# Second products four steps behind the first during the attention units, weights prepared three instructions a step, low-part products last

## The chip, the cores and the metric

One core of one Trainium2 chip runs the whole kernel. The time is the device time of one execution in microseconds (us); lower is better. TensorE (PE) does the matrix products, VectorE (DVE), ScalarE (ACT) and GpSimd (POOL) the elementwise work, SyncE (SP) issues the transfers. Each engine takes its instructions in the order in which the program gives them.

## What is computed

A decaying linear attention over 2 batches, 8 heads, 768 positions and 64 columns, and then two pairs of dense layers (512 to 2048 to 512) on its 1536 rows. In short, from the reference:

```python
state = gamma * state + outer(k[:, :, t], v[:, :, t])      # per head, for each t
y[:, :, t] = scale * q[:, :, t] @ state
h = x @ w_in;  g = max(h, 0) + log1p(exp(-abs(h)));  x = g @ w_out        # first pair
h = x @ w_in;  g = s * max(h, 0)**2 + b;             out = g @ w_out      # second pair
```

## The kernel before, in words

**Attention.** The sequence is cut into 12 chunks of 128 positions; a *unit* n is half the heads of chunk n // 2, so there are 24. For each unit PE makes the scores (`att_scores`, line 168), DVE multiplies them with the decay mask (line 172, tile `a`), and PE makes the output and the state's update (`att_out`, line 184). ACT copies the output as rounded high part into `xh` (line 216), DVE takes the rest into `xl` (line 222), adds up the state (lines 237 and 239), ACT copies that (lines 248 and 255).

**Layers.** Every number is held as a high and a low part, and a product of two such numbers is three products: high by high, high by low, low by high. A *step* s takes one block of 128 hidden columns (f4 of 4 in a group) for 512 rows (j of 3): `h_mm(s)` (line 313) is 12 products into one PSUM bank, the first products. `act_0` to `act_lo` make the activation of it (DVE line 322, ACT line 333, DVE line 338, ACT line 356 into `gh`, POOL or DVE line 360 into `gl`). `acc_mm` (line 376) is the second products, 12 of them, three into each of four banks (`acc01` is one tile of two banks, `acc2` and `acc3` are one each); four steps of a group add up in the same banks. After the fourth, `take_out` copies the four banks out (for the first group on ACT, line 382), and the next group may only then begin in them. There are 96 steps.

**Weights.** A tile of weights arrives as one transfer of 512 KB (`raw`, issued by `load_next` on SP in the third of its four preparing instructions) and is prepared by `split_w`: DVE instructions on lines 277, 281, 286 and 292, an ACT square on line 284, then ACT copies the high part `wh` (line 106) and POOL subtracts for the low part `wl` (line 109). The first four pieces are the first-product weights of f4 = 0 to 3, used by steps 0 to 3; then come the second-product weights in the same order. `fill(n)` issues the next n of these pieces, four to a tile.

**Order.** It is written out by hand. Units 0 to 7 run first (two tiles of weights are prepared there). Then eight steps carry two units each: steps 0 to 2 by `early` (first products, unit, scores, unit, scores, `fill(4)` at the end), steps 3 to 7 by `mixed`, which also has the second products of step s - 3 between the two units (`LAG_U = 3`) and calls `fill(2)` twice. In `early` the second unit's output lies in bank `acc3` and half of the scores in `acc01`. After the units one step's second products are made up, and the steady steps follow, 88 of them, each with the first products of s and the second products of s - 2 (`LAG`).

First products of a step up to 7 always use one bank `h`, so `h_mm(s + 1)` can start when `act_2(s)` (DVE, line 338) has read it. The weights' pool holds six tiles of each kind, the pool `raw` four transfers, the pool of `gh` and `gl` LAG_U + 1 pairs.

Of the kernel before, what the change touches and what calls it, by code (L numbers as in the profile page):

```python
# [13 lines left out]
P = 128  # L14
# [10 lines left out]
KC = DM // P  # L25
NF = DFF // P
FG = 4
# [4 lines left out]
WARM = {"first": 6, "u0": 3, "s2": 1}  # L32
FIRST, SECOND = (0, 1), (2, 3)
LAG = 2
LAG_U = 3
TINY_SQ = float.fromhex("0x1.44p-30")
HF = 2
HP = NP // HF
# [7 lines left out]
def tile_retention_mlps(ctx: ExitStack, tc: tile.TileContext, qk, kv, w1, w2, sb, consts, out):  # L46
    nc = tc.nc
# [2 lines left out]
    inp = ctx.enter_context(tc.tile_pool(name="inp", bufs=NIN))  # L50
    scp = ctx.enter_context(tc.tile_pool(name="scaled", bufs=2))
    ap_ = ctx.enter_context(tc.tile_pool(name="att", bufs=3))
    rawp = ctx.enter_context(tc.tile_pool(name="raw", bufs=4))
    dp = ctx.enter_context(tc.tile_pool(name="dec", bufs=2))
    wp = ctx.enter_context(tc.tile_pool(name="w", bufs=RING))
    gp = ctx.enter_context(tc.tile_pool(name="g", bufs=LAG_U + 1))
    tp = ctx.enter_context(tc.tile_pool(name="t", bufs=2))
    ps_acc = ctx.enter_context(tc.tile_pool(name="ps_acc", bufs=1, space=bass.MemoryType.PSUM))
    ps_h = ctx.enter_context(tc.tile_pool(name="ps_h", bufs=1, space=bass.MemoryType.PSUM))
    ps_y = ctx.enter_context(tc.tile_pool(name="ps_y", bufs=1, space=bass.MemoryType.PSUM))  # L60
    ps_s = ctx.enter_context(tc.tile_pool(name="ps_s", bufs=1, space=bass.MemoryType.PSUM))

    def bank(pool, tag):
        return pool.tile([P, 512], F32, tag=tag, name=tag)

    def sums():

        t = ps_acc.tile([P, 2, 512], F32, tag="acc01", name="acc01")
        return [t[:, 0], t[:, 1], bank(ps_acc, "acc2"), bank(ps_acc, "acc3")], t
# [14 lines left out]
    xh = [cp.tile([P, KC, TT], F32R, tag=f"xh{j}", name=f"xh{j}") for j in range(NTILE)]  # L84
    xl = [cp.tile([P, KC, TT], F32R, tag=f"xl{j}", name=f"xl{j}") for j in range(NTILE)]
# [10 lines left out]
    def word():  # L96
        if fill.at >= LAG_U:
            return dp.tile([P, DM], F32, tag="wx", name="wx", bufs=1)
        return ac[2]
# [201 lines left out]
    steps = [(la, g, j, f4) for la in range(2) for g in range(NG) for j in range(NTILE) for f4 in range(FG)]  # L301
    h_t, l_t, gg_t, acc_t = {}, {}, {}, {}

    def h_mm(s, part):
        la, g, j, f4 = steps[s]
        wh, wl = w_t[la * NF + g * FG + f4, 0]
        if part == 0:
            h_t[s] = bank(ps_h, "h") if s < SB or s % 2 else bank(ps_y, "y")
        ps = h_t[s]
        for cc in (0, 1) if part == 0 else (2, 3):  # L310
            wa, wb = (w[:, cc * P : (cc + 1) * P] for w in (wh, wl))
            for i, (l, r) in enumerate(((wa, xh), (wa, xl), (wb, xh))):
                nc.tensor.matmul(  # L313
                    ps, l, r[j][:, cc, :], start=cc == 0 and i == 0, stop=cc == KC - 1 and i == 2
                )

    def act_0(s):
        ps = h_t[s]
# [43 lines left out]
    def acc_mm(s, banks):  # L362
        la, g, j, f4 = steps[s]
        wh, wl = w_t[la * NF + g * FG + f4, 1]
        gh, gl = gg_t[s]
        if (la, g, j) not in acc_t:
            acc_t[la, g, j] = sums()[0] if acc_t else ac
        for cc in banks:
            cs = slice(cc * P, (cc + 1) * P)
            ps = acc_t[la, g, j][cc]  # L370
            if la == 0:
                ops = ((wh[:, cs], gh), (wh[:, cs], gl), (wl[:, cs], gh))
            else:
                ops = ((gh[:, cs], wh), (gh[:, cs], wl), (gl[:, cs], wh))
            for i, (l, r) in enumerate(ops):
                nc.tensor.matmul(ps, l, r, start=f4 == 0 and i == 0, stop=f4 == FG - 1 and i == 2)  # L376

    def take_out(s, cc):
        la, g, j, f4 = steps[s]
# [17 lines left out]
    SB = (NU - N0) // HF  # L397
# [5 lines left out]
    def slot_free(w, i):  # L403
# [6 lines left out]
            if x[0] >= FG  # L410
            else (-2, 2 * (x[0] + (LAG_U if x[1] else 0)) + x[1])
        ),
# [5 lines left out]
    def load_next():  # L418
        x = next(loads, None)
        if x:  # L420
            load_w(*x)
# [53 lines left out]
    def out_of(y):  # L475
        return y[:, :HC], y[:, HC : HC + HP * D]
# [3 lines left out]
    def fill(n):  # L480

        for _ in range(n):
            if not left[0]:
                if nxt[0] is None or fill.at < slot_free(*nxt[0]):
                    return
                work[0] = split_w(*nxt[0], pause=False)
                nxt[0] = next(splits, None)
                left[0] = 4
            next(work[0], None)
            left[0] -= 1  # L490

    with tc.manual_schedule():
        fill.at = -1
        nc.scalar.preload_act_table_set("softplus")
        nc.vector.memset(zero, 0.0)
        nc.vector.memset(st, 0.0)
        nc.vector.memset(cu[:, 0:1], 0xC0000000)
        nc.vector.memset(cu[:, 1:2], 29)
        load_qk(0)
        nc.sync.dma_start(out=cst[:, :CG], in_=consts[:, :CG])  # L500
        load_kv(0)
        nc.sync.dma_start(out=cst[:, CG:], in_=consts[:, CG:])
        load_qk(1)
        load_kv(1)
        load_qk(2)
        load_next()
        load_kv(2)
        load_qk(3)
        load_kv(3)

        def warm(bank, key):
            for _ in range(WARM[key]):
                nc.tensor.matmul(bank[:, 0:P], zero[:, 0:P], zero[:, P : 2 * P], start=True, stop=True)

        ys = [bank(ps_h, "h"), bank(ps_y, "y")]
        warm(ac[3], "first")
        scale_q(0)
        scale_v(0)
        score_to(2, lent)
        warm(ac[3], "u0")  # L520
        for n in range(N0):
            if n >= len(ys):
                ys.append(bank(*((ps_h, "h"), (ps_y, "y"))[n % 2]))
            unit(n, out_of(ys[n]))
            if n == 1:
                load_next()
                load_next()
                nc.sync.dma_start(out=sbt, in_=sb)
                warm(ac[3], "s2")

            score_to((2, 4, 5, 6, 7, 8, 9, 10)[n], lent)
            fill((0, 0, 0, 1, 1, 1, 1, 4)[n])

        def early(s):

            fill.at = s
            n = N0 + HF * s
            h_mm(s, 0)
            h_mm(s, 1)
            act_0(s)  # L540
            unit(n, out_of(bank(ps_y, "y")), lambda: act_1(s))
            score_to(n + 3, lent)
            act_2(s)
            act_3(s)
            unit(n + 1, out_of(ac[3]))
            act_hi(s)
            score_to(n + 4, lent)
            fill(4)
            act_lo(s, nc.gpsimd)

        def mixed(s):

            old = s - LAG_U
            fill.at = s
            n = N0 + HF * s
            h_mm(s, 0)
            h_mm(s, 1)
            act_0(s)
            unit(n, out_of(bank(ps_y, "y")), lambda: act_1(s))
            score_to(n + 3, own)  # L560
            act_2(s)
            act_3(s)
            act_hi(s)
            fill(2)
            acc_mm(old, FIRST)
            acc_mm(old, SECOND)
            unit(n + 1, out_of(bank(ps_y, "y")))
            score_to(n + 4, own)
            act_lo(s, nc.gpsimd)
            if steps[old][3] == FG - 1:  # L570
                for cc in range(KC):
                    take_out(old, cc)
            fill(2)

        for s in range(SB):
            (early if s < LAG_U else mixed)(s)
        for old in range(SB - LAG_U, SB - LAG):
            acc_mm(old, FIRST)
            acc_mm(old, SECOND)
        fill(left[0])  # L580
        work = iter(())
        for s in range(SB, NS + LAG):
            run, old, prev = s < NS, s - LAG, s <= NS
            takes = steps[old][3] == FG - 1
            late = work
            work = split_next(s + 1) if run and not takes else iter(())
            if run:
                h_mm(s, 0)
                h_mm(s, 1)
                act_0(s)  # L590
            if prev and s > SB:
                act_3(s - 1)
            go(work, 2)
            if run:
                acc_mm(old, FIRST)
                if takes:
                    take_out(old, 0)
                    take_out(old, 1)
                act_1(s)
            if prev and s > SB:  # L600
                act_hi(s - 1)
            if run:
                act_2(s)
            go(late, 1)
            if prev and s > SB:
                act_lo(s - 1)
            if run:
                acc_mm(old, SECOND)
                if takes:
                    take_out(old, 2)  # L610
                    take_out(old, 3)
            go(work, 2)

        for banks in (FIRST, SECOND[:1], SECOND[1:]):
            for old in (NS - 2, NS - 1):
                acc_mm(old, banks)
            for cc in banks:
                take_out(NS - 1, cc)
# [70 lines left out]
```

## Time and profile before

| | us |
|---|---|
| median of three runs | 586.97 (586.72 to 587.11) |
| the profiled execution | 587.33 |
| its span, first to last instruction | 585.2 |
| TensorE busy | 574.6 (98%) |
| VectorE, ScalarE, GpSimd busy | 452.4, 223.1, 134.9 |

The profile is one execution. The timeline lists instructions with their start, their duration and, in square brackets, how long the engine had been idle and which instruction ended that. The chain of waits follows the work that ended last back to its beginning. A product's duration in the timeline is longer than the step from one product to the next, because products overlap.

### The profile page before, as it was taken

The numbers are of one execution on the slowest core, as the hardware profiler recorded it, in microseconds if no ns is written. First come the engines' busy times: TensorE is split into PE (matmuls) and PEld (weight loads), VectorE is DVE, ScalarE is ACT, GpSimd is POOL, SyncE is SP. The second block draws the span as 40 slices with busy tenths as digits, with TensorE's granted clock in tenths as the row PEclk, the third lists the DMA queues.
The fourth block names the chain that finished last, engine by engine and source line by source line (L and its number), as shares of the span: only waits on it lengthen the run. The fifth ranks groups of instructions, "written<-read, shape, count | busy, mean of one in ns | idle before, by whom it ended". The sixth has DMA issues, their size and how long they took to land.

```text
span 585.2 us, 7908 instructions
## 1 busy us (share of the span) xinstructions
PE 574.6 (98%) x3028; PEld 472.7 (81%) x3028; DVE 452.4 (77%) x692; ACT 223.1 (38%) x441; POOL 134.9 (23%) x110
## 2 busy tenths in 40 slices
PE   8899999999999999999999999999999999999997
PEld 7776778888888888888778888888888888888885
DVE  4888665679999997899869897878778876874553
ACT  3655653443333333333534532333333332332121
POOL 3447632021021120121433420121101110110000
PEclk9999999999999999999999999999999999999999
DMA  8985212222222221222212221222112122000111
GB/s 328 416 302 198 73 38 71 73 73 73 72 73 72 73 72 37 72 73 72 73 37 73 61 83 45 64 72 91 54 38 96 48 72 67 6 1 0 73 72 73
DMA packets 14868, 50.57 MB, mean 86 GB/s; under 512 B 1776, under 2 KB 1776, under 8 KB 14832
## 3 DMA queue, kind: packets, MB, share of 16 engines
q1 hardware_dynamic: 14832, 50.08, 24.9%
q8 instruction: 24, 0.39, 0.3%
q14 instruction: 12, 0.10, 0.1%
HBM read 46.93 MB, written 3.15 MB: 86 GB/s over the span
## 4 chain that ended last, share of the span: by engine, by line
PE 91%; DVE 3%; DMA 2%; ACT 1%; POOL 1%; issue 1%; SPq 1%; POOLq 0%; DVEq 0%
PE acc L376 44%; PE h L313 23%; PE y L313 20%; PE y L184 2%; DMA qk<-qk 2%; PE s L168 1%; POOL wl L109 0%; DVE gl L360 0%; ACT xh L106 0%; DVE a L172 0%; DVE xa L386 0%; DVE t L338 0%; SPq L128 0%; ACT t L333 0%; DVE acc L286 0%
## 5 line engine op out<-in xcount | busy, mean ns | idle before, releaser
L109 POOL TENSOR_TENSOR wl<-wm,wh 128x512 fp32r<-128x512 f32 x64 | 84.0, 1312 | 362.3 <-ACT wh L106 336.4
L360 DVE TENSOR_TENSOR gl<-t,gh 128x512 fp32r<-128x512 f32 x88 | 85.0, 966 | 6.3 <-ACT gh L356 6.3
L313 PE MATMUL h<-xh,wh 128*128 128x512 f32 x208 | 81.9, 394 | 1.5 <-DVE t L338 1.1
L313 PE MATMUL h<-xh,wl 128*128 128x512 f32 x208 | 81.2, 390 | 0.6 <-POOL wl L109 0.6
L313 PE MATMUL h<-xl,wh 128*128 128x512 f32 x208 | 81.0, 389 | 0.0
L376 PE MATMUL acc<-gl,wh 128*128 128x512 f32 x192 | 75.0, 391 | 0.7 <-DVE gl L360 0.7
L376 PE MATMUL acc<-gh,wh 128*128 128x512 f32 x192 | 75.4, 393 | 0.0
L376 PE MATMUL acc<-gh,wl 128*128 128x512 f32 x192 | 74.9, 390 | 0.5 <-POOL wl L109 0.5
L376 PE MATMUL acc<-wh,gl 128*128 128x512 f32 x192 | 74.7, 389 | 0.0
L376 PE MATMUL acc<-wl,gh 128*128 128x512 f32 x192 | 74.7, 389 | 0.0
L376 PE MATMUL acc<-wh,gh 128*128 128x512 f32 x192 | 74.7, 389 | 0.0
L333 ACT ACTIVATE t<-t 128x512 f32<-128x512 f32 x48 | 30.2, 630 | 101.1 <-DVE t L322 101.1
L386 DVE TENSOR_TENSOR xa<-acc,xa 128x512 f32<-128x512 f32 x72 | 46.3, 682 | 28.8 <-PE acc L376 28.8
L313 PE MATMUL y<-xh,wh 128*128 128x512 f32 x176 | 68.5, 389 | 0.0
L313 PE MATMUL y<-xl,wh 128*128 128x512 f32 x176 | 68.5, 389 | 0.0
L313 PE MATMUL y<-xh,wl 128*128 128x512 f32 x176 | 68.5, 389 | 0.0
L356 ACT ACTIVATE gh<-t 128x512 fp32r<-128x512 f32 x96 | 59.7, 622 | 3.8 <-DVE t L338 2.3
L338 DVE SCALAR_TENSOR_TENSOR t<-h,t 128x512 f32<-128x512 f32 x52 | 35.6, 684 | 23.0 <-ACT t L327 14.6
L327 ACT ACTIVATE t<-h 128x512 f32<-128x512 f32 x24 | 14.3, 597 | 87.7 <-PE h L313 87.7
L313 PEld LDWEIGHTS h<-xh,wh 128*128 128x128 f32 x208 | 39.1, 188 | 10.6 <-DVE t L338 1.5
L327 ACT ACTIVATE t<-y 128x512 f32<-128x512 f32 x24 | 14.3, 597 | 84.6 <-PE y L313 84.6
L313 PEld LDWEIGHTS h<-xh,wl 128*128 128x128 f32 x208 | 39.0, 187 | 9.3 <-POOL wl L109 1.1
(84 smaller groups left out, 953.7 us busy)
## 6 DMA issues: line engine op xcount, KB each, us to landing
raw<-w SPq DMA_DIRECT2D x64, 512.0 KB, 3.7
qk<-qk SPq DMA_DIRECT2D x12, 512.0 KB, 7.9
kv<-kv SPq DMA_DIRECT2D x12, 512.0 KB, 8.0
out<-xa SPq DMA_DIRECT2D x12, 256.0 KB, 2.0
cst<-consts SPq DMA_DIRECT2D x1, 518.0 KB, 4.2
cst<-consts SPq DMA_DIRECT2D x1, 256.0 KB, 5.9
sbt<-sb SPq DMA_DIRECT2D x1, 1.0 KB, 9.9
```

Source lines behind the costliest of these rows:

```text
L109: lo_eng.tensor_tensor(out=lo, in0=src, in1=hi.bitcast(F32), op=ALU.subtract)
L168: nc.tensor.matmul(banks[:, h, i * C : (i + 1) * C], t[r, 1, p], t[r, 0, p], start=True, stop=True)
L184: nc.tensor.matmul(y[to][h * D : (h + 1) * D, cols], l, r, start=h not in done, stop=True, skip_group_check=True)
L313: nc.tensor.matmul(ps, l, r[j][:, cc, :], start=cc == 0 and i == 0, stop=cc == KC - 1 and i == 2)
L327: nc.scalar.activation(t1, ps, AF.Relu)
L333: nc.scalar.activation(l_t[s], l_t[s], AF.Softplus)
L338: nc.vector.scalar_tensor_tensor(out=t2, in0=ps, scalar=0.0, in1=l_t[s], op0=ALU.max, op1=ALU.add if steps[s][0] == 0 else ALU.mult,)
L356: nc.scalar.activation(gg_t[s][0], l_t[s], AF.Copy)
L360: (eng or nc.vector).tensor_tensor(out=gl, in0=l_t.pop(s), in1=gh.bitcast(F32), op=ALU.subtract)
L376: nc.tensor.matmul(ps, l, r, start=f4 == 0 and i == 0, stop=f4 == FG - 1 and i == 2)
L386: nc.vector.tensor_tensor(out=dst, in0=ps, in1=dst, op=ALU.add)
```

## The change

- `LAG_U` is 4: step 3 becomes an `early` step, steps 4 to 7 are `mixed`, and two steps' second products (4 and 5) are made up after the units instead of one.
- `early` calls `fill(3)` instead of `fill(4)`, `mixed` calls `fill(2)` and `fill(3)` instead of twice `fill(2)`. The sum up to step 7 is 32 in both.
- `h_mm` and `acc_mm` make the products with the weights' low part last: in `h_mm` eight products with `wh` and then four with `wl`; in `acc_mm` for the banks of one call first two products to each bank, then the third.
- In `mixed` the four banks are one call of `acc_mm` instead of two.
- The pool `raw` has three buffers instead of four, and one `load_next` in front of the loop goes; the pool of `gh` and `gl` has five pairs.

```diff
-LAG_U = 3
+LAG_U = 4
...
-    rawp = ctx.enter_context(tc.tile_pool(name="raw", bufs=4))
+    rawp = ctx.enter_context(tc.tile_pool(name="raw", bufs=3))
...
-    def h_mm(s, part):
+    def h_mm(s):
...
-        for cc in (0, 1) if part == 0 else (2, 3):
-            wa, wb = (w[:, cc * P : (cc + 1) * P] for w in (wh, wl))
-            for i, (l, r) in enumerate(((wa, xh), (wa, xl), (wb, xh))):
-                nc.tensor.matmul(
-                    ps, l, r[j][:, cc, :], start=cc == 0 and i == 0, stop=cc == KC - 1 and i == 2
-                )
+        ops = [(w, r, cc) for cc in range(KC) for w, r in ((wh, xh), (wh, xl))]
+        ops += [(wl, xh, cc) for cc in range(KC)]
+        for i, (w, r, cc) in enumerate(ops):
+            nc.tensor.matmul(
+                ps, w[:, cc * P : (cc + 1) * P], r[j][:, cc, :], start=i == 0, stop=i == len(ops) - 1
+            )
...
+        parts = ((0, 1), (2,)) if len(banks) > 1 else ((0, 1, 2),)
+        for some in parts:
+            for cc in banks:
...
+                    ops = ((gh[:, cs], wh), (gl[:, cs], wh), (gh[:, cs], wl))
+                for i in some:
...
             if n == 1:
                 load_next()
-                load_next()
...
             score_to(n + 4, lent)
-            fill(4)
+            fill(3)
             act_lo(s, nc.gpsimd)
...
             fill(2)
-            acc_mm(old, FIRST)
-            acc_mm(old, SECOND)
+            acc_mm(old, FIRST + SECOND)
             unit(n + 1, out_of(bank(ps_y, "y")))
...
-            fill(2)
+            fill(3)
```

DVE's instructions from the second half of step 1 to the start of step 2. In the names, `a` is a unit's masked scores, `wm` a tile of weights before it is parted, `t1` and `t2` the activation; `raw_207` is the transfer of the fourth tile of weights in the first listing, `raw_348` in the second. Before:

```order
L338 SCALAR_TENSOR_TENSOR t2_551<-h_516,t1_529 128x512
L222 TENSOR_TENSOR xl1_104<-acc3_111,xh1_101 128x2x128
L172 TENSOR_TENSOR a_574<-acc01_109,cst_94 128x512
L277 TENSOR_SCALAR acc2_110<-raw_207 128x512
L281 SCALAR_TENSOR_TENSOR acc2_110<-raw_207,cu_96,acc2_110 128x512
L286 SCALAR_TENSOR_TENSOR acc2_110<-raw_207,cu_96,acc2_110 128x512
L292 SCALAR_TENSOR_TENSOR wm_578<-wm_578,acc2_110 128x512
L322 TENSOR_SCALAR t1_602<-h_589 128x512
```

Now (here `wm_503` is the third tile):

```order
L338 SCALAR_TENSOR_TENSOR t2_546<-h_511,t1_524 128x512
L222 TENSOR_TENSOR xl1_104<-acc3_111,xh1_101 128x2x128
L172 TENSOR_TENSOR a_569<-acc01_109,cst_94 128x512
L292 SCALAR_TENSOR_TENSOR wm_503<-wm_503,acc2_110 128x512
L277 TENSOR_SCALAR acc2_110<-raw_348 128x512
L281 SCALAR_TENSOR_TENSOR acc2_110<-raw_348,cu_96,acc2_110 128x512
L322 TENSOR_SCALAR t1_594<-h_581 128x512
```

The last preparing instruction of the third tile, line 292, stood at the end of step 0 and stands now behind the last masked scores of step 1; the one of the fourth tile stood at the end of step 1 and comes now behind the masked scores of step 2, with line 286 ahead of it.

TensorE at the end of the units, where the next group first uses the four banks (an `acc01` with a new number; `acc2_110` and `acc3_111` are the group before). `h_1088` is step 7's first products, `y_1053`, `y_1103` and `y_1118` are outputs of units 21, 22 and 23. Before, from the end of step 7's first products:

```order
L313 MATMUL h_1088<-xh1_101,wl0_577 128x512
L184 MATMUL y_1103<-q2_1021,st_97 64x128 x4
L184 MATMUL y_1103<-a_1027,kv_764 64x128 x4
L376 MATMUL acc01_1127<-gh_827,wh1_659 128x512
L376 MATMUL acc01_1127<-gl_828,wh1_659 128x512
L376 MATMUL acc01_1127<-gh_827,wl1_660 128x512
```

Now, from the end of the second products of step 3:

```order
L377 MATMUL acc2_110<-gh_710,wl1_958 128x512
L377 MATMUL acc3_111<-gh_710,wl1_958 128x512
L184 MATMUL y_1118<-q2_1000,st_97 64x128 x4
L184 MATMUL y_1118<-a_1053,kv_733 64x128 x4
L377 MATMUL acc01_1142<-gh_799,wh1_657 128x512
L377 MATMUL acc01_1142<-gl_800,wh1_657 128x512
```

And ScalarE there, where `xa0` are the copies out of the four banks. Before:

```order
L216 ACTIVATE xh2_102<-y_1053 128x2x128
L248 ACTIVATE st_97<-sm_98 64x2x64 x2
L382 ACTIVATE xa0_106<-acc01_109 128x512 x2
L382 ACTIVATE xa0_106<-acc2_110 128x512
L382 ACTIVATE xa0_106<-acc3_111 128x512
L106 ACTIVATE wh0_1034<-wm_1037 128x512
L216 ACTIVATE xh2_102<-y_1103 128x2x128
```

Now:

```order
L106 ACTIVATE wh0_1056<-wm_1059 128x512
L216 ACTIVATE xh2_102<-y_1118 128x2x128
L385 ACTIVATE xa0_106<-acc01_109 128x512 x2
L385 ACTIVATE xa0_106<-acc2_110 128x512
L385 ACTIVATE xa0_106<-acc3_111 128x512
```

Between the last unit ahead of the four copies and the next group's first second products stood the first products of step 7 and unit 22; now nothing stands there, and the copies follow on ScalarE right behind the copy of unit 23's output.

## Rows read from the trace of the kernel before

**Rows 1.** The page, part 1: busy time, share of span, instructions.

```profile
PE 574.6 (98%) x3028; PEld 472.7 (81%) x3028; DVE 452.4 (77%) x692; ACT 223.1 (38%) x441; POOL 134.9 (23%) x110
```

**Rows 2.** Waits of TensorE in the steady steps: total us, times, longest.

```profile
PE acc L376 <- DVE gl L360: 0.7, 2, 0.3
```

**Rows 3.** Timeline of PE: start, duration, instruction, count, [idle before <- what ended it].

```profile
24.07 0.50 PE L313 MATMUL h<-xh,wh 128*128 128x512 f32 x1 [0.45 <-ACT wh L106]
...
25.43 0.50 PE L313 MATMUL h<-xh,wl 128*128 128x512 f32 x1 [0.63 <-POOL wl L109]
...
31.73 0.50 PE L313 MATMUL h<-xh,wh 128*128 128x512 f32 x1
...
38.47 0.50 PE L313 MATMUL h<-xh,wh 128*128 128x512 f32 x1 [0.37 <-DVE t L338]
...
41.92 0.40 PE L184 MATMUL y<-v,kv 128*64 128x64 f32 x8
...
45.16 0.50 PE L313 MATMUL h<-xh,wh 128*128 128x512 f32 x1 [0.73 <-DVE t L338]
...
51.28 0.50 PE L376 MATMUL acc<-gh,wl 128*128 128x512 f32 x1 [0.53 <-POOL wl L109]
```

**Rows 4.** Timeline of DVE, steps 0 to 3.

```profile
30.85 0.68 DVE L338 SCALAR_TENSOR_TENSOR t<-h,t 128x512 f32<-128x512 f32 x1
...
38.33 0.41 DVE L222 TENSOR_TENSOR xl<-acc,xh 128x256 fp32r<-128x256 f32 x1
...
38.66 0.68 DVE L172 TENSOR_TENSOR a<-acc,cst 128x512 f32<-128x512 f32 x1
...
43.29 0.29 DVE L237 COPY sm<-y 128x128 f32<-128x128 f32 x1 [0.37 <-ACT xh L216]
...
46.15 0.68 DVE L277 TENSOR_SCALAR acc<-raw 128x512 uint32<-128x512 uint32 x1
...
47.66 0.76 DVE L286 SCALAR_TENSOR_TENSOR acc<-raw,cu,acc 128x512 uint32<-128x512 uint32 x1
...
48.52 0.69 DVE L292 SCALAR_TENSOR_TENSOR wm<-wm,acc 128x512 f32<-128x512 f32 x1
...
52.79 1.67 DVE L281 SCALAR_TENSOR_TENSOR wx<-raw,cu,wx 128x512 uint32<-128x512 uint32 x1
```

**Rows 5.** Timeline of ACT, steps 1, 6 and 7.

```profile
37.50 0.38 ACT L216 ACTIVATE xh<-acc 128x256 fp32r<-128x256 f32 x1 [0.22 <-PE acc L184]
...
42.35 0.63 ACT L106 ACTIVATE wh<-wm 128x512 fp32r<-128x512 f32 x1 [2.72 <-DVE wm L292]
...
85.72 2.07 ACT L382 ACTIVATE xa<-acc 128x512 f32<-128x512 f32 x4
...
92.94 0.38 ACT L216 ACTIVATE xh<-y 128x256 fp32r<-128x256 f32 x1 [1.04 <-PE y L184]
```

**Rows 6.** Chain of waits, mixed steps and first steady step: start, us, what.

```profile
55.74 2.97 PE h L313 x12
...
58.71 1.25 PE y L184 x24
...
59.96 0.65 PE s L168 x8
...
92.90 2.94 PE acc L376 x12
...
95.84 2.72 PE y L313 x12
```

**Rows 7.** Stretches at the end: us, engines busy (instructions), clock, DMA, GB/s.

```profile
581.00:582.00 1.00, 0.25 (x2) 0.00 (x0) 0.69 (x1) 0.00 (x0) 0.00 (x0) 1.00 0.98 379
...
584.50:585.00 0.50, 0.00 (x0) 0.00 (x0) 0.00 (x0) 0.00 (x0) 0.00 (x0) 1.00 0.00 0
...
585.00:585.20 0.20, 0.00 (x0) 0.00 (x0) 0.00 (x0) 0.00 (x0) 0.00 (x0) 0.61 0.00 0
```

**Rows 8.** The page, part 6: transfers, KB each, us from issue to landing.

```profile
raw<-w SPq DMA_DIRECT2D x64, 512.0 KB, 3.7
```

More of the change, by code (lines that the diff above doesn't have):

```diff
@@ L302, in tile_retention_mlps @@
     h_t, l_t, gg_t, acc_t = {}, {}, {}, {}
-    def h_mm(s, part):
+    def h_mm(s):
         la, g, j, f4 = steps[s]
         wh, wl = w_t[la * NF + g * FG + f4, 0]
-        if part == 0:
-            h_t[s] = bank(ps_h, "h") if s < SB or s % 2 else bank(ps_y, "y")
+        h_t[s] = bank(ps_h, "h") if s < SB or s % 2 else bank(ps_y, "y")
         ps = h_t[s]
-        for cc in (0, 1) if part == 0 else (2, 3):
-            wa, wb = (w[:, cc * P : (cc + 1) * P] for w in (wh, wl))
-            for i, (l, r) in enumerate(((wa, xh), (wa, xl), (wb, xh))):
-                nc.tensor.matmul(
-                    ps, l, r[j][:, cc, :], start=cc == 0 and i == 0, stop=cc == KC - 1 and i == 2
-                )
+        ops = [(w, r, cc) for cc in range(KC) for w, r in ((wh, xh), (wh, xl))]
[4 more added lines that the diff above has]
+            )
     def act_0(s):
@@ L367, in acc_mm @@
             acc_t[la, g, j] = sums()[0] if acc_t else ac
[L368 to L376, printed above, removed]
+        parts = ((0, 1), (2,)) if len(banks) > 1 else ((0, 1, 2),)
+        for some in parts:
+            for cc in banks:
+                cs = slice(cc * P, (cc + 1) * P)
+                if la == 0:
+                    ops = ((wh[:, cs], gh), (wh[:, cs], gl), (wl[:, cs], gh))
+                else:
+                    ops = ((gh[:, cs], wh), (gl[:, cs], wh), (gh[:, cs], wl))
+                for i in some:
+                    nc.tensor.matmul(
+                        acc_t[la, g, j][cc], *ops[i], start=f4 == 0 and i == 0, stop=f4 == FG - 1 and i == 2
+                    )
     def take_out(s, cc):
@@ L537, in early @@
             n = N0 + HF * s
-            h_mm(s, 0)
-            h_mm(s, 1)
+            h_mm(s)
             act_0(s)
@@ L555, in mixed @@
             n = N0 + HF * s
-            h_mm(s, 0)
-            h_mm(s, 1)
+            h_mm(s)
             act_0(s)
@@ L587, in tile_retention_mlps @@
             if run:
-                h_mm(s, 0)
-                h_mm(s, 1)
+                h_mm(s)
                 act_0(s)
```

## The prediction

> **What bounds the kernel now.** I read the page's first part first. TensorE is busy 574.6 of 585.2 us [rows 1], so only what moves its products or its gaps counts. The chain of waits shows where it is merely busy: in the steady steps twelve products take 2.72 us, without a break from step 8 on (95.84) to the end [rows 6], and TensorE's waits there come to 0.7 us in two places, on a `gl` of the first pair [rows 2]. The other gaps lie between the start of the layers and step 3's second products. The timeline of PE has five of them: 0.45 and 0.63 us in step 0 (`wh`, then `wl` of the first tile), 0.37 and 0.73 us at the first products of steps 2 and 3 (line 338, the reader of their bank), 0.53 us at the first second products (`wl`) [rows 3], together 2.71 us. That is all the change could give there, 0.46% of the time; so the question is what it does to these stretches and to the end of the units, and what it costs.
>
> **Step 0, low parts last.** The wait for `wh` at 24.07 stays: nothing ahead of it changes. The wait for `wl` ended at 25.43 [rows 3]; eight products now come first, and twelve from the units' time take 2.97 [rows 6], so the ninth is due at about 24.07 + 2.97 x 8/12 = 26.0: that gap goes. Step 1's first products gain less, since they need line 338 of step 0 (30.85 + 0.68 = 31.53 [rows 4], and a handover from engine to engine, 0.02 to 0.06 each, such as 0.04 from the unit that ends at 92.90 to its copy at 92.94 [rows 5, 6]): 31.59 if DVE moves not at all, against 31.73 [rows 3], and at most 0.4 earlier. I take 31.5.
>
> **Step 1, three instructions instead of four.** The order shows line 292 of the third tile behind the last masked scores of step 1, and `wh` of that tile is needed by step 2's very first product. Step 1 takes PE from 31.73 to 38.47 - 0.37 = 38.10 [rows 3], 6.37, so PE is free at 31.5 + 6.37 = 37.9. The chain beside it, 0.23 earlier than in the trace: ACT's copy of the step's second unit, 37.50 - 0.23 = 37.27, lasts 0.38 [rows 5], to 37.65; `xl`, 0.33 until the next instruction (38.33 to 38.66 [rows 4]), to 38.0; masking, 0.60, to 38.6; line 292, 0.69 [rows 4], to 39.3; `wh` on ACT, 0.63 [rows 5], with handovers to 39.95. Step 2's first products start at 40.0 instead of 38.47: 1.5 later, with TensorE idle 2.1. Before, DVE's four instructions a step were what step 2 waited for (0.37); that goes, and 2.1 comes in its place, because the work that used to lie under the whole of step 1 now begins when step 1 ends.
>
> **Step 2.** PE needs 45.16 - 0.73 - 38.47 = 5.96 for it [rows 3] and is free at 46.0. The fourth tile has two instructions left, lines 286 and 292, again behind the step's last masked scores. The first unit's products end 41.92 + 0.40 - 38.47 = 3.85 after the step's start [rows 3], so at 43.85; ACT's copy, 0.38 and handovers, 44.3; from the state's sum to the end of the second masking DVE needs 46.15 - 43.29 = 2.86 [rows 4], to 47.15; lines 286 and 292, 0.86 from one to the next and 0.69, to 48.7; `wh` 0.63, and 0.1 of handovers: 49.4, against 45.16. Step 3 starts 4.2 later, behind an idle stretch of 3.4.
>
> **Step 3 as an early step.** Products 2.97, then twice a unit of 1.25 and scores of 0.65 [rows 6]: 6.77, so step 4's first products start at 56.2; its waits (line 338, `xh` and `xl` of units 8 to 15) are met inside. Before it was 55.7 [rows 6]: only 0.5 later, but twelve second products now are still to be made, which stood there before with their gap of 0.53.
>
> **Four mixed steps and the made-up ones.** From 55.74 to the end of the units at 92.90 there are 37.16 us with the same bursts in both [rows 6]; DVE gets one instruction more in each half step, where it waits for units anyway. Low parts last hides POOL's `wl` under eight products here. Then the new place: the four copies of the first group's banks come behind the copy of unit 23's output on ACT, and PE has nothing between unit 23 and the next group's first second product, which writes `acc01`, one tile for two of these copies. Price: 0.06 to ACT and 0.28 until its next instruction, then two of four copies that took 2.07 (0.48 from one to the next, the second 0.63) [rows 5], and 0.06 back: 1.5. The third and fourth copies end 0.5 and 1.0 later, under the six products on `acc01`. Before, step 7's products and unit 22 lay between (4 us), and nothing waited. Behind it come two bursts, 2.94 and 2.72 [rows 6], where one of 2.94 stood: 2.7 more. Step 8 starts 0.5 + 1.5 + 2.7 = 4.7 later.
>
> **From step 8 on.** Forty instructions of preparing are done in both, so the queues stand alike. The order of the products costs nothing that a row shows: second products change their bank at every third product and first products stay in one, and both take 2.72 in the steady steps of the chain, with one weight load for each product (3028 and 3028 [rows 1]). The copies of `acc01` in the steady steps come behind all six products either way. In the second pair `gl` moves from third to second product, 0.23 earlier; no wait on it shows there, and the two that show are in the first pair [rows 2], where it was second already. I take 0. One transfer less is under way early: the fourth tile's is now issued when line 286 of the first tile is done, and it is read at the end of step 1, more than 10 us later; none of the five gaps was a transfer's, so nothing is gained either. On SP the transfers of the chunks move one place forward, and they wait for their own buffers. Later each transfer is issued two and a half tiles ahead instead of three and a half; a steady step prepares at most one tile, so that is over 10 us against the 3.7 from issue to landing [rows 8]. Without that cover a late tile would hold up PE by what is missing.
>
> **Sum.** Span 585.2 + 4.7 = 589.9; the profiled execution 587.33 + 4.7 = 592.0. It lies 0.36 above the median of the runs, so I expect **591.7**, 0.8% slower.
>
> **Bounds.** Step 1's start: 0.1 earlier or 0.4. The wait on the copies: nothing if PE does not reach it first (590.2), 1.5 as taken. DVE's line 281 once took 1.67 where line 286, of the same kind, takes 0.76 [rows 4]; if one such excess of 0.9 fell on each of the two late chains, 593.5. From below: if step 1's gain were 0.4 and the handovers of both chains shorter by 0.1 each, 591.3.
>
> **Rivals.** *The weights come in time.* If the two late tiles were ready when TensorE is, steps would follow at 31.5, 37.9, 43.8, and step 4 at 50.6, 5.1 earlier than before; the made-up second products (2.7) and the wait on ACT (1.5) remain: 0.9 faster, 586.1, which counts as no change. If that wait, too, found other work in front of it, 2.4 faster, 584.6: this is the side on which the change is a gain, and it decides at lines 292 of the third and fourth tile, which must end 0.7 us before the last scores of steps 1 and 2 do. For it speaks that DVE has less to do per step; against it the order, which puts them behind those very scores. *The change does only half*: the wait at step 2 is there, and step 3's is as short (2.1): 590.4, inside the range.
>
> *The clock falls in the gap.* After the last product, which ends at 581.3, the granted clock was still 1.00 (2.4 GHz) up to 585.0; in the last 0.2 us it is 0.61, a mean of that level and the lower one of 1.2 GHz [rows 7]. So an idle TensorE does lose its clock here. The idle stretch before step 3 is 3.4 us by the sum, with one of 2.1 a step ahead of it and products in between. If it fell, the twelve products behind it would take up to twice 2.97, and at the most the whole of step 3 (6.77) twice as long: 594.7 with one burst, 598.5 at the far end. The Trainium skill, "TensorE: Matmul & The Clock Gate", section "HAM oscillation — how this bites in real kernels", says that idle gaps between groups of products make the chip throttle TensorE again, so that the next group starts at the lower clock; it speaks against a change that makes few long gaps of many short ones. By that rule the time would be the 594.7; the row shows the fall at the end alone, and no idle stretch of such length between products is in this trace.
>
> **How the numbers follow.** Forecast with its bounds 0.83, the clock's fall 0.08, weights in time with the wait 0.05, without it 0.04. The range 589.6 to 594.0 leaves out the two cases of weights in time and most of the clock's. A measurement of this kernel tells 0.2% (1.2 us) from no change: faster 0.04, same 0.05, slower 0.91.
>
> **What would show it.** In the timeline of PE: step 0 without a wait for `wl`; idle of about 2 us before step 2's first product and 3.4 before step 3's, both ended by ACT's `wh`; no gap at the first second products; 1.5 us ended by ACT's copy (line 385) behind unit 23; step 8 at about 100.5 instead of 95.8, and from there to the end the same length. It is wrong if `wh` of the third tile is ready before step 1's last scores end, if the copies are done before PE comes, or if a clock below 1.00 shows near 50 us.

## The result and the profile after

| | before | changed |
|---|---|---|
| median, us | 586.92 | 594.87 (594.75 to 595.0) |
| ratio | 1 | 1.0131 (1.0119 to 1.0143) |
| span of the profiled execution, us | 585.2 | 592.6 |
| start of step 0's products to start of step 8's, us | 24.07 to 95.84 | 23.78 to 103.25 |
| from there to the end of the span, us | 489.4 | 489.3 |

The change is 1.3% slower, 8.0 us, where 4.7 were forecast and 594.0 was the range's upper end. The whole loss of the profiled execution lies between the start of step 0 and the start of step 8: 79.5 us instead of 71.8. From there to the end the two kernels agree within 0.1 us. Of all the runs below one is left out of its median: 721.29 us, with three transfers, at a mean granted clock of 0.753.

The page of the changed kernel, span, part 1 and the clock row of part 2 (40 slices of 14.8 us, in tenths):

```profile
span 592.6 us, 7904 instructions
...
PE 577.7 (97%) x3028; PEld 475.8 (80%) x3028; DVE 454.5 (77%) x692; ACT 223.0 (38%) x441; POOL 134.0 (23%) x110
...
PEclk9988999999999999999999999999999999999999
```

TensorE is busy 3 us longer than in [rows 1] with the same products, and two slices have a clock of 8 tenths. These are the slices from 29.6 to 59.3 us, about the time of steps 1 to 3.

The timeline of TensorE, all instructions between 20 and 110 us with idle time marked ahead of them (columns as in [rows 3]):

```profile
23.78 0.50 PE L313 MATMUL h<-xh,wh 128*128 128x512 f32 x1 [0.45 <-ACT wh L106]
...
31.06 0.50 PE L313 MATMUL h<-xh,wh 128*128 128x512 f32 x1 [0.47 <-DVE t L338]
...
39.56 0.50 PE L313 MATMUL h<-xh,wh 128*128 128x512 f32 x1 [2.15 <-ACT wh L106]
...
50.50 0.62 PE L313 MATMUL h<-xh,wh 128*128 128x512 f32 x1 [3.40 <-ACT wh L106]
...
97.51 0.50 PE L377 MATMUL acc<-gh,wh 128*128 128x512 f32 x1 [1.46 <-ACT xa L385]
```

This answers to [rows 3]. The waits for `wl` are gone. In the place of 0.37 and 0.73 us on line 338 stand 2.15 and 3.40 us on ACT's `wh`, and 1.46 us on ACT's copies came new. The sum had 2.1, 3.4 and 1.5. Step 1, whose weights come in time, now waits 0.47 us on line 338: it starts 7.28 us behind step 0 instead of 7.66, so of the 0.63 us of the lost wait for `wl` 0.38 are gained.

ScalarE and VectorE at the end of steps 1 and 2, from their timelines (line 172 masks the last scores of the step, 286 and 292 prepare the weights, 106 is `wh`):

```profile
37.57 0.68 DVE L172 TENSOR_TENSOR a<-acc,cst 128x512 f32<-128x512 f32 x1
...
38.17 0.68 DVE L292 SCALAR_TENSOR_TENSOR wm<-wm,acc 128x512 f32<-128x512 f32 x1
...
38.88 0.63 ACT L106 ACTIVATE wh<-wm 128x512 fp32r<-128x512 f32 x1 [1.04 <-DVE wm L292]
...
47.72 0.68 DVE L172 TENSOR_TENSOR a<-acc,cst 128x512 f32<-128x512 f32 x1
...
48.31 0.75 DVE L286 SCALAR_TENSOR_TENSOR acc<-raw,cu,acc 128x512 uint32<-128x512 uint32 x1
...
49.09 0.69 DVE L292 SCALAR_TENSOR_TENSOR wm<-wm,acc 128x512 f32<-128x512 f32 x1
...
49.81 0.63 ACT L106 ACTIVATE wh<-wm 128x512 fp32r<-128x512 f32 x1 [0.54 <-DVE wm L292]
```

The chain is the one of the order: masking, then line 292 (behind line 286 in the second case), then `wh`, and 0.05 and 0.06 us later the first product at 39.56 and 50.50.

What the sum did not have stands in the chain of waits: the bursts of twelve products behind the two idle stretches, with one on either side.

```profile
31.06 3.01 PE h L313 x12
...
39.56 4.61 PE h L313 x12
...
50.50 4.62 PE h L313 x12
...
58.92 2.94 PE h L313 x12
```

4.61 and 4.62 us instead of 3.01 and 2.94. And the stretches of one microsecond around the first and the second (columns as in [rows 7]):

```profile
38.00:39.00 1.00, 0.00 (x0) 0.00 (x0) 0.97 (x3) 0.12 (x1) 0.00 (x0) 1.00 1.03 410
...
40.00:41.00 1.00, 1.00 (x5) 0.81 (x4) 0.37 (x1) 0.08 (x1) 1.00 (x2) 0.74 1.01 410
...
41.00:42.00 1.00, 1.00 (x4) 0.72 (x4) 0.00 (x0) 0.00 (x0) 1.00 (x1) 0.50 0.80 328
...
43.00:44.00 1.00, 1.00 (x4) 0.49 (x2) 0.00 (x0) 0.00 (x0) 1.00 (x2) 0.55 0.00 0
...
44.00:45.00 1.00, 1.00 (x19) 0.83 (x18) 0.69 (x1) 0.00 (x0) 0.35 (x1) 1.00 0.00 0
...
48.00:49.00 1.00, 0.00 (x0) 0.00 (x0) 1.00 (x2) 0.98 (x4) 0.00 (x0) 1.00 0.98 340
...
49.00:50.00 1.00, 0.00 (x0) 0.00 (x0) 0.93 (x3) 0.46 (x2) 0.00 (x0) 1.00 0.18 70
...
50.00:51.00 1.00, 0.50 (x2) 0.40 (x3) 0.51 (x1) 0.45 (x1) 0.48 (x1) 0.86 0.67 225
...
51.00:52.00 1.00, 1.00 (x4) 0.81 (x3) 0.00 (x0) 0.00 (x0) 1.00 (x2) 0.50 0.81 168
...
53.00:54.00 1.00, 1.00 (x4) 0.75 (x3) 0.00 (x0) 0.00 (x0) 1.00 (x2) 0.50 0.66 262
...
55.00:56.00 1.00, 1.00 (x19) 0.95 (x20) 0.69 (x1) 0.00 (x0) 0.27 (x1) 1.00 0.01 4
```

No product runs from 38 to 39 and from 48 to 50, and the clock is still 1.00 there. It falls when products run again, in the microsecond from 40 and in the one from 50, to 0.50, which is 1.2 GHz, and is back at 1.00 in those from 44 and 55.

### The profile page after: what moved, and what is told of

Read it like the earlier page. It is cut to its first block, busy times and chain, and to the rows that moved or that the text cites. A ratio compares the mean times of both kernels' runs of the same rounds, so it can differ in the third digit from the quotient of the medians.

```text
span 592.6 us, 7904 instructions
## 1 busy us (share of the span) xinstructions
PE 577.7 (97%) x3028; PEld 475.8 (80%) x3028; DVE 454.5 (77%) x692; ACT 223.0 (38%) x441; POOL 134.0 (23%) x110
## 4 chain that ended last, share of the span: by engine, by line
PE 91%; DVE 4%; DMA 2%; ACT 2%; SPq 1%; issue 0%; DVEq 0%
PE acc L377 44%; PE h L313 24%; PE y L313 19%; PE y L184 2%; DMA qk<-qk 2%; PE s L168 1%; DVE a L172 1%; DVE wm L292 0%; DVE t L338 0%; DVE gl L360 0%; ACT wh L106 0%; ACT xh L106 0%; PE acc L184 0%; DVE xl L222 0%; DVE acc L286 0%
## 5 line engine op out<-in xcount | busy, mean ns | idle before, releaser
L313 PE MATMUL h<-xh,wh 128*128 128x512 f32 x208 | 83.2, 400 | 6.5 <-ACT wh L106 6.0
L313 PE MATMUL h<-xl,wh 128*128 128x512 f32 x208 | 82.7, 398 | 0.0
L377 PE MATMUL acc<-wl,gh 128*128 128x512 f32 x192 | 59.4, 389 | 0.0
L377 PE MATMUL acc<-gh,wl 128*128 128x512 f32 x192 | 58.5, 389 | 0.0
L313 PE MATMUL h<-xh,wl 128*128 128x512 f32 x208 | 56.5, 394 | 0.0
L313 PEld LDWEIGHTS h<-xh,wh 128*128 128x128 f32 x208 | 39.7, 191 | 15.8 <-ACT wh L106 6.6
L313 PE MATMUL y<-xh,wl 128*128 128x512 f32 x176 | 47.1, 389 | 0.0
L313 PEld LDWEIGHTS h<-xl,wh 128*128 128x128 f32 x208 | 39.8, 191 | 8.1
```

The lines of the kernel that those rows point to most:

```text
L313: nc.tensor.matmul(ps, w[:, cc * P : (cc + 1) * P], r[j][:, cc, :], start=i == 0, stop=i == len(ops) - 1)
L377: nc.tensor.matmul(acc_t[la, g, j][cc], *ops[i], start=f4 == 0 and i == 0, stop=f4 == FG - 1 and i == 2)
```

## The experiments

The theory: two tiles of weights come late because their last instructions stand behind the last masked scores; the idle stretches that follow cost themselves and a fall of the clock each; the copies cost 1.5 us; the order of products and the fewer transfers cost nothing. The rivals: that the fourth step of lag is what costs; that the slow bursts come from GpSimd and the transfers beside them; that the order of products has a price.

### Four instructions a step again

```diff
 (early)
-            fill(3)
+            fill(4)
 (mixed, second call)
-            fill(3)
+            fill(2)
```

> The changed kernel with four preparing instructions at the end of an early step and twice two in a mixed one, as before; all else stays changed. If the late weights are the cause of both idle stretches (2.15 and 3.40 us) and these of the clock's falls, the stretches shrink to about 0.4 and 0.8 us on line 338, the clock stays at 1.00, and of the 7.95 us over the kernel before some 7 go: 4.3 of idle time and 3.3 of slow products, so about 587.3. If instead the fourth step of lag costs the most (step 3 without second products, two steps made up), it stays above 591.

Measured: 587.30 us against 587.17 of the kernel before on the same chip, ratio 1.0003 (0.9994 to 1.0012). Over the kernel before, 7.95 us have become 0.13, so 7.8 us hang on these two numbers. The waits of TensorE from 20 us on, in total, times and longest:

```profile
PE h L313 <- DVE t L338: 1.7, 3, 0.7
...
PE acc L377 <- ACT xa L385: 1.5, 1, 1.5
...
PE acc L377 <- DVE gl L360: 0.6, 2, 0.3
...
PE h L313 <- ACT wh L106: 0.4, 1, 0.4
```

The waits for `wh` in steps 2 and 3 are gone and the clock is 1.00 in this profile; the copies' 1.5 us stand as before. The lag of four steps, with the low parts last, comes out even. As an estimate: low parts last gain 1.0 us (below) and the copies cost 1.5, which leaves nothing clear of the noise for the fourth step of lag itself.

### Products of zeros in the idle stretches

```diff
 (early, ahead of h_mm)
+            h_t[s] = bank(ps_h, "h")
+            for _ in range((0, 0, 4, 6)[s]):
+                nc.tensor.matmul(h_t[s][:, 0:P], zero[:, 0:P], zero[:, P : 2 * P], start=True, stop=True)
```

`zero` holds zeros, and `h_mm` then writes to the bank taken here instead of taking one.

> The changed kernel with products of zeros into bank h, which the step's own first product clears, ahead of the first products of steps 2 (four) and 3 (six), in the time in which TensorE waits for wh; the weights come no earlier. If the slow twelve products of these steps (4.61 us instead of 2.97) come from the clock that fell after the idle stretches, both bursts take 2.97 again, the clock is 1.00 throughout, and the time is 594.9 - 2 x 1.64 = 591.6. If the bursts are slow for another reason (GpSimd and transfers are at work beside them), it stays at 594.9. If the products of zeros run on past the arrival of wh, up to 0.5 us each comes back.

Measured: 591.79 us, ratio 1.0079 (1.0064 to 1.0095). The chain of waits has both bursts, and the stretches of one microsecond show what ran beside them (columns as in [rows 7]):

```profile
39.84 3.04 PE h L314 x12
...
49.21 3.04 PE h L314 x12
```

```profile
41.00:42.00 1.00, 1.00 (x6) 0.82 (x5) 0.00 (x0) 0.00 (x0) 1.00 (x2) 1.00 0.91 373
...
51.00:52.00 1.00, 1.00 (x6) 0.69 (x4) 0.00 (x0) 0.00 (x0) 1.00 (x2) 1.00 1.04 410
```

Step 2's first products start 15.8 us behind step 0's, as in the changed kernel (39.84 - 24.05 here, 39.56 - 23.78 there), step 3's 25.2 behind it against 26.7, which is step 2's faster burst; GpSimd is as busy and the transfers are as dense beside them as in the changed kernel, and the bursts are at full speed, with a clock of 1.00. So the slow bursts are the clock, and the clock fell because TensorE stood still. Each kernel against the kernel before on its own chip, 7.95 us become 4.62: 3.3 go that way, and what is left is the forecast's sum of 4.7.

The same in one of the two places only, six ahead of step 3, then four ahead of step 2:

> Products of zeros ahead of step 3 alone; the idle stretch of 2.15 us ahead of step 2 stays. If each idle stretch costs its own fall of the clock, step 2's burst stays at 4.6 us and step 3's is 2.97: 594.9 - 1.65 = 593.2. If an idle stretch of 2.15 us is too short to cost one and the first fall had another cause, also 593.2 but with the clock at 1.00; if only the two together do it, 591.6.

> The changed kernel with products of zeros ahead of step 2 alone (four); the idle stretch of 3.40 us ahead of step 3 stays. If each stretch costs its own fall, step 2's burst takes 2.97 and step 3's stays slow: 593.2, or up to 1.7 more where the second fall lasts twice as long, as it did in the profile of e3_copies.

Measured: zeros ahead of step 3 alone 593.71 us (ratio 1.0114, 1.0101 to 1.0128); ahead of step 2 alone 593.36 (1.0105, 1.0088 to 1.0122). Over the kernel before on the same chip that is 6.8 and 6.2 us, so the one takes 1.2 away and the other 1.7, where both together take 3.3; the first came out 0.5 us above what was expected. The bursts of steps 2 and 3, first in the one, then in the other, from the chains of waits:

```profile
40.47 4.50 PE h L314 x12
...
51.30 3.01 PE h L314 x12
```

```profile
39.71 3.03 PE h L314 x12
...
49.07 5.37 PE h L314 x12
```

Each stretch costs its own fall. In the second of these profiles the clock fell while TensorE still stood idle, and the burst took 5.37 us:

```profile
46.00:47.00 1.00, 0.00 (x0) 0.00 (x0) 1.00 (x4) 0.88 (x4) 0.00 (x0) 1.00 0.78 258
...
48.00:49.00 1.00, 0.00 (x0) 0.00 (x0) 0.97 (x2) 0.61 (x1) 0.00 (x0) 0.50 0.21 41
...
49.00:50.00 1.00, 0.93 (x2) 0.83 (x3) 0.08 (x1) 0.02 (x1) 0.91 (x1) 0.50 0.96 246
```

### The copies ahead of unit 23

```diff
 (mixed)
+            if steps[old][3] == FG - 1:
+                for cc in range(KC):
+                    take_out(old, cc)
             unit(n + 1, out_of(bank(ps_y, "y")))
             score_to(n + 4, own)
             act_lo(s, nc.gpsimd)
-            if steps[old][3] == FG - 1:
-                for cc in range(KC):
-                    take_out(old, cc)
```

> The changed kernel with the four copies out of the banks (take_out of step 3) issued ahead of unit 23 instead of behind it; nothing else. If the wait of 1.46 us behind unit 23 is these copies alone, it goes and the time is 593.4; the copy of unit 23's output comes later on ACT, which must not hold up step 8's first products, or part of it comes back (594 and more).

> Products of zeros in the two idle stretches (as in e2_filler) and the copies ahead of unit 23 (as in e3_copies) together. With the clock held up, the 1.46 us of the copies must show in the time, which in e3_copies the clock's differing falls hid: 591.8 - 1.5 = 590.3. If the copies' wait is only moved elsewhere, 591.8.

Alone: 593.76 us, but its runs lie between 591.71 and 595.08, and in the profile the wait of 1.46 us is gone while the burst of step 3 takes longer than in the changed kernel:

```profile
40.09 4.54 PE h L313 x12
...
50.95 5.49 PE h L313 x12
```

So this run alone could not price the copies: the clock's second fall lasted longer here, and the mean granted clock of its four runs differs, 0.991 to 0.996. With the products of zeros as well, which hold the clock, it can: 590.30 us (590.13 to 590.45; ratio 1.0056, 1.0042 to 1.0070). Over the kernel before on the same chip that is 3.4 us, where the zeros alone left 4.6; the profiled executions, 589.7 and 588.2 us, differ by 1.5, which is the wait of 1.46, and that wait is gone from the timeline.

### One part alone: low parts last, and three transfers

> The kernel before with one part of the change: products with the weights' low part last, in h_mm and acc_mm, four banks in one call in mixed. If the order of products has no price of its own, the waits for wl (0.63 and 0.53 us) go, the one on line 338 takes some of it, and the time is 0.6 to 0.9 below the kernel before, about 586.2. If changing banks or operands oftener costs even 1 ns a product, it is 2 us slower, 588.5 or more.

```diff
-            for i, (l, r) in enumerate(((wa, xh), (wa, xl), (wb, xh))):
...
+        ops = [(w, r, cc) for cc in range(KC) for w, r in ((wh, xh), (wh, xl))]
+        ops += [(wl, xh, cc) for cc in range(KC)]
...
```

The new order in `acc_mm`, with the four banks in one call in `mixed`, is in this version too.

Measured: 586.13 us, ratio 0.9984 (0.9975 to 0.9993): faster by 1.0 us. No cost of the order shows, and the gain is near the two waits for `wl`, 0.63 and 0.53 us.

> The kernel before with one part of the change: three transfers of weights ahead instead of four, one load less in unit 1. If transfers are covered throughout, the time is that of the kernel before within 0.2%. If a late transfer holds a step up, single gaps of TensorE show in the steady steps, or the chunks' transfers move and units wait: slower by what is missing.

```diff
-    rawp = ctx.enter_context(tc.tile_pool(name="raw", bufs=4))
+    rawp = ctx.enter_context(tc.tile_pool(name="raw", bufs=3))
...
             if n == 1:
                 load_next()
-                load_next()
```

Measured: 587.12 us in nine runs, ratio 1.0003 (0.9994 to 1.0012): no difference.

### The place in the queue

```diff
 (early)
+            fill(1)
             unit(n + 1, out_of(ac[3]))
             act_hi(s)
             score_to(n + 4, lent)
-            fill(3)
+            fill(2)
```

> The changed kernel with three preparing instructions a step as it has, but the first of them (line 292 of the third tile, in step 1) ahead of the step's second unit instead of behind its last masked scores. If the place behind the last scores is what makes the third tile late, the idle stretch ahead of step 2 falls from 2.15 to about 1.2 us; ahead of step 3, where line 286 goes ahead and line 292 stays behind, it stays above 3. Time 593.9, or 592.2 if the clock then doesn't fall at step 2. If the number of instructions alone counted, both stretches would stay.

Measured: 593.05 us (592.38 to 593.09; ratio 1.0098, 1.0083 to 1.0113). The two first products from the timeline:

```profile
38.88 0.50 PE L313 MATMUL h<-xh,wh 128*128 128x512 f32 x1 [1.08 <-ACT wh L106]
...
48.23 0.50 PE L313 MATMUL h<-xh,wh 128*128 128x512 f32 x1 [3.41 <-ACT wh L106]
```

With line 292 of the third tile ahead of the second unit the stretch falls from 2.15 to 1.08 us, and behind it the burst takes 3.02 at a clock of 1.00. So with three instructions a step, it is the place behind the last scores that makes the third tile late. The profiled run, 592.38 at a mean clock of 0.996, is close to the 592.2 expected without the fall at step 2; the three others, 593.04 to 593.09, have 0.993.

For the fourth tile the place is not all. Line 286 went ahead of the second unit there, line 292 still stands behind the scores, and the stretch stays at 3.41 instead of 3.40 us. VectorE's timeline in step 2, at its last idle time ahead of line 292:

```profile
43.18 0.29 DVE L237 COPY sm<-y 128x128 f32<-128x128 f32 x1 [0.55 <-ACT xh L216]
...
46.69 0.68 DVE L292 SCALAR_TENSOR_TENSOR wm<-wm,acc 128x512 f32<-128x512 f32 x1
```

From 43.18 to the end of line 292 VectorE works without a pause, and moving line 286 within that stretch ends it no sooner. What is late there is all that step 2 still has to do for this tile, two instructions more than in the kernel before, where they stood at the end of step 1. Fewer instructions a step and their place act together here; no run separates them for this tile.

### A version below both

The changed kernel with `fill(4)`, one of the four ahead of an early step's second unit, and the copies ahead of unit 23:

```diff
 (early)
+            fill(1)
             unit(n + 1, out_of(ac[3]))
...
 (mixed: the copies as above)
-            fill(3)
+            fill(2)
```

> The changed kernel with four preparing instructions a step again, one of them ahead of an early step's second unit, and the copies ahead of unit 23. Late weights, the clock's falls and the wait on the copies are gone, low parts stay last: TensorE waits only for line 338 in steps 1 to 3. From e1_fill4 (587.3) 1.5 less: 585.8, below both kernels. If line 338 comes later by the copies or the moved instruction, 586.3.

Measured: 585.47 us, ratio 0.9974 (0.9963 to 0.9984). TensorE's waits from 20 us on:

```profile
PE h L313 <- DVE t L338: 1.3, 3, 0.6
...
PE acc L377 <- DVE gl L360: 0.7, 2, 0.3
...
PE h L313 <- ACT wh L106: 0.4, 1, 0.4
```

Of the five gaps of the kernel before, the two for `wl` are gone, and those on line 338 come to 1.3 us over three steps.

## Why the prediction was wrong, point by point

- **The stretches before the change, the place of the loss**: right. From step 8 on the two kernels agree within 0.1 us.
- **Low parts last**: right. The waits for `wl` went, and the order had no price (one part alone: 1 us faster).
- **Late tiles in steps 2 and 3**: right in mechanism and size, 2.15 and 3.40 us for 2.1 and 3.4; the order of the queue and the durations of the rows were enough for it.
- **The copies behind unit 23**: right, 1.46 for 1.5, and shown by moving them.
- **Sum without the clock**: right. With the clock held up the kernel is 4.6 us over the one before, and in its profile step 8 starts 4.6 us later behind step 0; 4.7 were forecast.
- **The rival "The clock falls in the gap"**: this is the step that failed. It was named, with the right mechanism, but got a chance of 0.08, stood at nothing in the sum, and was priced once, for step 3 alone. The clock fell twice, also behind the 2.1 us that the text had only mentioned, and each fall cost a burst 1.6 us (4.61 and 4.62, against 3.04 with zeros): 3.2 us, which with the 4.6 left when the clock is held is 7.8 of the 7.95 measured. The prediction's own sign of being wrong, a clock below 1.00 near 50 us, is there. That the rival's 594.7 lies near the result is chance: it had one fall at 3.0 instead of two at 1.6.

For its small chance the prediction gives no more than one row. [rows 7] showed the clock at 1.00 for 3.7 us after the last product. To count 3.4 us as likely safe by that was an argument from one fall at the end of a program, behind which no product came. The runs show the other side: behind the stretch of 2.15 us the clock fell after products had been running again for the better part of a microsecond. With the copies ahead, and with zeros ahead of step 3, it fell within the stretch of the same length. So the idle stretch need not be as long as what the end of the program showed, and one does not always see the fall by looking at the stretch alone. The rule of the Trainium skill, "TensorE: Matmul & The Clock Gate", section "HAM oscillation — how this bites in real kernels", that idle gaps between groups of products throttle TensorE, so that the next group starts at the lower clock, agrees with this case's trace in the first half at both stretches: those of 2.15 and 3.40 us cost 3.2 us beyond themselves. In the second half the changed kernel differs, where the group behind the first stretch started at 1.00 and lost the clock 0.9 us later; with the copies ahead both groups did start at 0.50.

## What to carry to other kernels

An instruction's place in an in-order queue can cost more than the instruction itself: three preparing instructions a step instead of four moved the last one behind work that depends on the step's end, and turned a hidden chain into an idle stretch on TensorE. Price an idle stretch of TensorE like the 2.15 us here as itself and as a slower burst behind it, with a chance that is not small, and count every such stretch by itself. To find out whether a burst is slow by the clock, keep TensorE busy with products nobody needs and change nothing else.

## What the runs showed of the chip

- The granted clock went to 0.50 behind TensorE's idle stretches of 2.15 us (three profiles: the changed kernel, the copies ahead, zeros ahead of step 3) and of 3.40 us (four: the changed kernel, the copies ahead, zeros ahead of step 2, line 292 moved), and stayed at 1.00 behind those of 1.06 to 1.57 us, some of which follow products of zeros. No run has a stretch in between, and none tests how much the work around a stretch matters.
- The fall came in some profiles while TensorE still stood idle (zeros ahead of step 2 alone, zeros ahead of step 3 alone, the copies ahead both times), in others only when products had run again (the changed kernel both times, line 292 moved); the burst behind it took 4.33 to 5.49 us instead of 3.0. How long it lasted differs between runs of one kernel: the runs with the copies ahead spread over 3.4 us, where the kernel before spreads over 1.0.
- Products of zeros by zeros, ten of them in two stretches, held the clock at 1.00, in both versions that had them.
